# A transformer block with window attention, rebuilt as a pipeline over four groups of 512 tokens, with 64-key score blocks of head pairs and softmax sums by a block-diagonal matmul

## The chip, the cores and the metric

The kernel runs on one core of one Trainium2 chip. The metric is device time in microseconds (us), as the median of several runs. The profile is of one execution; its span, from the first to the last instruction, is 1.7 to 2.1 us shorter than the time of the same run, in every run on record that has both. "Clock" is the mean clock that the throttle granted to the TensorE array, 1.00 being full speed. A run's state is called slow when it is over 1.5% above the fastest of its kernel; ratios use the fast runs alone. Experiments with changed kernels were timed beside the kernel before on the same chip, in three batches on three chips.

Engines: PE is TensorE (PEld its weight loads), ACT is ScalarE, DVE is VectorE, POOL is GpSimd, SP issues the DMAs. PSUM is the memory that matmuls write; an eviction copies from it.

## The reference

One block on 2048 tokens of 512 features: adaptive layer norm, causal attention with a window of 256 and 32 heads of 16, output projection and gated residual, a second adaptive norm, then an MLP that mixes along the *token* axis, again with norm, gate and residual. Cut to what matters:

```python
h = layernorm(x) * (1 + ca) + sa                # modulation from silu(c) @ w_mod
q, k, v = split_heads(h @ wqkv)                 # H = 32 heads of 16
scores = where((q_idx >= k_idx) & (q_idx - k_idx < 256), q @ k.T / 4, -1e9)
x = x + ga * (softmax(scores) @ v) @ wo
h = layernorm(layernorm(x) * (1 + cb) + sb)
u = gelu(einsum('sd,sf->df', h, w1) + b1)       # S = 2048 tokens -> F = 1792
x = x + gb * (u @ w2 + b2).T                    # F -> S
```

## The kernel before

Three stages follow each other. (1) Norm, transposes, value projection and the first query/key projection of all 2048 tokens. (2) Attention, in 8 passes (4 groups of 128 features, even and odd heads) over 16 key blocks of 128; the other 12 projections run in its background. (3) Output projection, norms and MLP, whose two products of 224 matmuls each are called B1 and B2 below. The core of stage 2 (cuts marked):

```python
pending_proj = [(4 * i, g8, tg) for i, (g8, tg) in enumerate(...)]   # 12 projections, one every 4 steps
...
for hs in range(8):                        # 8 passes: (g8, even or odd heads)
    for kb in range(NT):                   # 16 key blocks of 128
        et = epool.tile([P, 4, 3, P], DT.bfloat16, name="et")
        for a in range(2):                 # 4 heads x 3 query blocks: 2 exps of 128 x 768
            nc.scalar.activation(out=et[:, 2*a:2*a+2, 0:nr, :],
                in_=cur[a][:, :, 0:nr*P]..., func=ACT.Exp, scale=SCORE_SCALE)
        cur = emit_scores(ps_s, Ksel, QT[g8], kb + 1, ...)
        while pending_proj and pending_proj[0][0] <= att_step: ...   # 8 matmuls of 512 columns
        att_step += 1
        nc.vector.tensor_tensor(out=et[:, :, 0:3:2, :], ...)         # mask the two edge blocks
        for j in range(4):                 # values, 16 columns of ones beside them: the sums come free
            for kk in kks:
                nc.tensor.matmul(po[32*j:32*j+32, qi, :], lhsT=vaug_lhsT(kk, head), rhs=ering[kk]...)
        if qi == 3: ...                    # VectorE: cast, transpose, reciprocal, multiply, transpose
```

Each 128x768 exp has 3 query blocks of 128, of which the window needs 256 + 128/2 on average; the rest is masked to zero afterwards.

The softmax here doesn't subtract the row's maximum and nothing guards it: scores larger than these inputs give would overflow.

## Time and profile before

| | before |
|---|---|
| time, median of 3 runs before the prediction (4 with the next) | 408.64 us (411.1) |
| span of the profile | 404.0 us |
| stage 1, up to the first exp | 46.8 us |
| stage 2, up to the last value matmul | 222.8 us |
| stage 3 | 134.4 us |

The first view is the page of the kernel before: busy time of each engine, then the granted clock in tenths of full speed in 40 slices of 10.1 us, then three of the costliest groups (line, engine, operation, output and inputs, count | busy us, mean ns of one | idle before it and what ended most of that).

```profile
PE 350.6 (87%) x3713; PEld 168.9 (42%) x3713; DVE 279.5 (69%) x656; ACT 267.8 (66%) x426; POOL 8.7 (2%) x24
...
PEclk9999999699999655555555555569999999999997
...
L317 ACT ACTIVATE et<-pss 128x768 bf16<-128x768 f32 (+2 forms) x256 | 179.5, 779 | 30.4 <-PE psb L347 27.9
L329 DVE TENSOR_TENSOR et<-et,mask_661 128x1024 bf16<-128x1024 bf16 x112 | 75.3, 678 | 25.5 <-ACT et L317 25.0
L347 PE MATMUL psb<-et,VaugT 128*32 128x128 bf16 x1440 | 78.4, 276 | 1.8 <-DVE et L329 0.7
```

The exps are 256 instructions and 179.5 us of ScalarE. Of the 30.4 us that ScalarE sat idle just before an exp, 27.9 were ended by L347, the value matmul that stands ahead of the next scores in PE's queue. PE's own "busy" is no measure of its load, since matmuls overlap (those of 512 columns last 0.38 us in the records and start 0.216 us apart).

The second view cuts the kernel before into its three stages: from : to, length, busy us and instruction count of each engine, then clock, DMA share and GB/s.

```profile
0.00:46.80 46.80, 33.43 (x214) 17.08 (x215) 33.65 (x98) 25.41 (x48) 8.69 (x24) 1.00 0.53 158
46.80:269.60 222.80, 200.21 (x2980) 100.58 (x2978) 161.04 (x307) 185.11 (x270) 0.00 (x0) 0.68 0.01 2
269.60:404.00 134.40, 116.94 (x526) 51.24 (x521) 84.82 (x252) 57.24 (x109) 0.00 (x0) 0.97 0.33 126
```

Attention has ScalarE at 83% (185.11 of 222.80 us) and a mean clock of 0.68. The third view counts only the exps (L317) in stretches of attention of the kernel before.

```profile
46.00:100.00 54.00, 42.02 (x59) 0.94 0.01 2
100.00:145.00 45.00, 36.98 (x55) 0.87 0.01 2
145.00:200.00 55.00, 45.69 (x65) 0.50 0.01 2
200.00:260.00 60.00, 50.42 (x72) 0.50 0.01 2
```

Until about 135 us, projections of full array size fill PE's background and the clock is near 1. When they have run out, it is 0.50 to the end of attention. The exps are about as dense in both halves (0.82 of the time at 100 to 145 us, 0.84 at 200 to 260), from which I concluded, before the prediction, that the clock does not matter here.

### The profile page before, as it was taken

To read this page: it belongs to the slowest core of one execution; us is meant where nothing else is said; L and a number is where in the kernel's file an instruction comes from. 1 tells how busy PE (TensorE), PEld (TensorE's weight loads), DVE (VectorE), ACT (ScalarE), POOL (GpSimd) and SP (SyncE) were. 2 spreads that over 40 slices of the span, in tenths; PEclk is the share of its full clock that TensorE was granted. 3 is DMA by queue.
4 is the path that set the end of the run, shared out by engine and by line. 5 is a ranking of instruction groups with operands and counts; after the bars stand their busy time and mean duration, and the time that the engine had idled before them with its cause. 6 is when DMAs were issued, how large, how long until landed. Compare 5 with 4: busy or idle time off the path is not lost.

```text
span 404.0 us, 8898 instructions
## 1 busy us (share of the span) xinstructions
PE 350.6 (87%) x3713; PEld 168.9 (42%) x3713; DVE 279.5 (69%) x656; ACT 267.8 (66%) x426; POOL 8.7 (2%) x24
## 2 busy tenths in 40 slices
PE   0898997999998898988889988998996799899993
PEld 0543443444444444544444444533342344344441
DVE  6795676688978587757687666679996597522344
ACT  3486588788988888978788878859997554300000
POOL 8000000000000000000000000000000000000000
PEclk9999999699999655555555555569999999999997
DMA  7970000000000000000000000007900592001111
GB/s 221 357 152 0 2 2 2 2 2 2 2 2 2 3 2 2 2 2 2 2 2 2 2 2 2 2 2 287 408 34 0 205 412 112 0 6 48 53 54 53
DMA packets 17169, 24.70 MB, mean 61 GB/s; under 512 B 5096, under 2 KB 12776, under 8 KB 17128
## 3 DMA queue, kind: packets, MB, share of 16 engines
q1 hardware_dynamic: 17128, 24.13, 17.0%
q8 instruction: 29, 0.48, 0.5%
q14 instruction: 12, 0.10, 0.1%
HBM read 22.03 MB, written 2.10 MB: 60 GB/s over the span
## 4 chain that ended last, share of the span: by engine, by line
PE 55%; DVE 21%; ACT 18%; issue 5%; DMA 1%; SPq 0%; ACTq 0%; DVEq 0%
PE pss L289 13%; PE psb L347 13%; ACT et L317 12%; PE py L519 12%; PE pu L499 7%; PE psb L161 3%; DVE ln_stats L455 2%; PE psb L168 2%; DVE ln_stats L436 2%; PE psb L221 2%; DVE et L329 2%; ACT h1T L211 2%; DVE ln_stats L192 1%; PE psb L429 1%; ACT gelu_a L405 1%
## 5 line engine op out<-in xcount | busy, mean ns | idle before, releaser
L317 ACT ACTIVATE et<-pss 128x768 bf16<-128x768 f32 (+2 forms) x256 | 179.5, 779 | 30.4 <-PE psb L347 27.9
L329 DVE TENSOR_TENSOR et<-et,mask_661 128x1024 bf16<-128x1024 bf16 x112 | 75.3, 678 | 25.5 <-ACT et L317 25.0
L347 PE MATMUL psb<-et,VaugT 128*32 128x128 bf16 x1440 | 78.4, 276 | 1.8 <-DVE et L329 0.7
L347 PEld LDWEIGHTS <-VaugT 128*32 128x32 bf16 x1440 | 37.6, 110 | 40.4 <-issue 34.4
L519 PEld LDWEIGHTS <-w2r 128*128 128x128 bf16 x224 | 21.9, 98 | 28.0 <-issue 1.8
L161 PE MATMUL psb<-h1T,wqkv 128*128 128x512 bf16 x64 | 21.5, 398 | 1.2 <-DVE t_1654 L357 0.4
L168 PE MATMUL psb<-h1T,wqkv 128*128 128x512 bf16 x64 | 18.4, 384 | 1.9 <-DVE t_1101 L357 0.4
L499 PEld LDWEIGHTS <-w1r 128*128 128x128 bf16 x128 | 12.5, 98 | 16.6 <-issue 1.2
L221 PE MATMUL psb<-wqkv,h1T 128*128 128x512 bf16 x64 | 17.6, 401 | 1.9 <-ACT QT_196 L165 0.8
L289 PE MATMUL pss<-QT_198,KoT_206 32*128 32x128 bf16 x180 | 16.0, 297 | 3.1 <-ACT et L317 2.9
L289 PE MATMUL pss<-QT_199,KeT_203 32*128 32x128 bf16 x180 | 16.0, 296 | 2.7 <-ACT et L317 2.7
L289 PE MATMUL pss<-QT_198,KeT_202 32*128 32x128 bf16 x180 | 16.0, 296 | 2.7 <-ACT et L317 2.7
L289 PE MATMUL pss<-QT_199,KoT_207 32*128 32x128 bf16 x180 | 16.3, 297 | 2.4 <-ACT et L317 2.2
L289 PE MATMUL pss<-QT_197,KoT_205 32*128 32x128 bf16 x180 | 15.3, 286 | 3.2 <-ACT et L317 3.0
L398 PEld LDWEIGHTS <-w1r 128*128 128x128 bf16 x96 | 9.7, 101 | 19.7 <-issue 10.8
L417 ACT ACTIVATE gelu_sg<-gelu_inner 128x512 bf16<-128x512 bf16 x14 | 8.8, 630 | 11.9 <-DVE gelu_inner L413 11.9
L409 DVE SCALAR_TENSOR_TENSOR gelu_sq<-gelu_a 128x512 bf16<-128x512 bf16 x14 | 9.6, 687 | 7.3 <-ACT gelu_a L405 7.1
L289 PE MATMUL pss<-QT_196,KeT_200 32*128 32x128 bf16 x180 | 11.4, 220 | 3.2 <-ACT et L317 2.4
L289 PE MATMUL pss<-QT_196,KoT_204 32*128 32x128 bf16 x180 | 11.9, 228 | 0.4 <-ACT et L317 0.4
L289 PEld LDWEIGHTS <-KoT_207 32*128 32x128 bf16 x180 | 7.6, 115 | 10.6 <-issue 10.3
L289 PE MATMUL pss<-QT_197,KeT_201 32*128 32x128 bf16 x180 | 11.3, 217 | 0.5 <-ACT et L317 0.2
L289 PEld LDWEIGHTS <-KoT_206 32*128 32x128 bf16 x180 | 7.5, 115 | 9.9 <-issue 9.7
(523 smaller groups left out, 570.0 us busy)
## 6 DMA issues: line engine op xcount, KB each, us to landing
w1r<-in_B_w_dram SPq DMA_DIRECT2D x16, 448.0 KB, 9.0
w2r<-in_B_w_dram SPq DMA_DIRECT2D x14, 512.0 KB, 9.5
wmod<-in_w_mod_dram SPq DMA_DIRECT2D x6, 512.0 KB, 6.1
out_dram<-otile SPq DMA_DIRECT2D x16, 128.0 KB, 1.7
wqkv<-in_A_wqkv_dram SPq DMA_DIRECT2D x4, 384.0 KB, 6.2
wod<-in_A_wo_dram SPq DMA_DIRECT2D x4, 128.0 KB, 3.4
x_64<-in_A_x_dram SPq DMA_DIRECT2D x1, 128.0 KB, 2.1
x_65<-in_A_x_dram SPq DMA_DIRECT2D x1, 128.0 KB, 2.2
```

The source lines that it names most:

```text
L161: nc.tensor.matmul(pq[:], lhsT=wqkv[:, dc, g8 * P : (g8 + 1) * P], rhs=h1T[:, dc, tok], start=(dc == 0), stop=(dc == ND - 1),)
L168: nc.tensor.matmul(pk[:], lhsT=wqkv[:, dc, D + g8 * P : D + (g8 + 1) * P], rhs=h1T[:, dc, tok], start=(dc == 0), stop=(dc == ND - 1),)
L221: nc.tensor.matmul(pv[:], lhsT=h1T[:, dc, tb * P : (tb + 1) * P], rhs=wqkv[:, dc, 2 * D : 3 * D], start=(dc == 0), stop=(dc == ND - 1),)
L289: nc.tensor.matmul(pss[:, jj, r * P : (r + 1) * P], lhsT=Ksel[rows, kb * P : (kb + 1) * P], rhs=qt[rows, qb * P : (qb + 1) * P], start=Tru ...
L317: nc.scalar.activation(out=et[:, 2 * a : 2 * a + 2, 0:nr, :], in_=cur[a][:, :, 0 : nr * P].rearrange("p h (r q) -> p h r q", q=P), func=AC ...
L329: nc.vector.tensor_tensor(out=et[:, :, 0:3:2, :], in0=et[:, :, 0:3:2, :], in1=mask01[:].unsqueeze(1).to_broadcast([P, 4, 2, P]), op=ALU.mult,)
L347: nc.tensor.matmul(po[32 * j : 32 * j + 32, qi, :], lhsT=vaug_lhsT(kk, head), rhs=ering[kk][:, j, r, :], start=(idx == 0), stop=(idx == le ...
L398: nc.tensor.matmul(pu[:, i, :], lhsT=w1r[:, sc, fc * P : (fc + 1) * P], rhs=hb[sc][:], start=(sc == 0), stop=(sc == NT - 1),)
L409: nc.vector.scalar_tensor_tensor(out=sq[:], in0=a[:], scalar=GELU_C0, in1=a[:], op0=ALU.mult, op1=ALU.mult,)
L417: nc.scalar.activation(out=sg[:], in_=inner[:], func=ACT.Sigmoid, scale=GELU_C1)
L499: nc.tensor.matmul(pu[:, i, :], lhsT=w1r[:, sc, fc * P : (fc + 1) * P], rhs=hb[sc][:], start=(sc == 0), stop=(sc == NT - 1),)
L519: nc.tensor.matmul(py[:, tl, :], lhsT=w2r[:, fc, tb * P : (tb + 1) * P], rhs=guT[fc][:], start=(fc == 0), stop=(fc == NF - 1),)
```

## The change

Its intent: do not wait for all projections before attention; give ScalarE fewer and larger exps; let PE make the softmax sums in the layout in which they are needed, so that VectorE need not transpose; do the norms of finished tokens while attention still runs.

- **Groups.** Four groups of 512 tokens. Group G's attention runs while group G+1's projections and group G-1's output projection and norms are issued between its steps.
- **Scores.** A block is 64 keys of an even head on partitions 0 to 63 and of the odd head of the pair on 64 to 127. One row-tiled matmul (on 32 of the array's 128 rows; the value and sum matmuls are column-tiled, on 32 of its columns) makes scores for both heads, up to 320 queries wide. Blocks are packed into chunks of 512 columns: 76 steps of 2 exps of 128x1024 (128x768 in four of them).
- **Sums.** A second matmul with a block-diagonal matrix of ones (scaled by 2^-32) puts each head's sum on the partitions of its values; ScalarE inverts it as exp(-ln z); one VectorE multiply finishes.
- **Engines.** Norm application, value evictions and residuals move to VectorE; the masked key copies to GpSimd; GELU becomes one activation; 1/sqrt becomes exp(-0.5 ln), so attention needs a single activation table.

The diff, cut to its core:

```diff
-            for j in range(4): ... 12 score matmuls of 128 columns, 2 exps of 128x768
+CHUNKS = [[(-2, 0, 3, 0), (-4, 0, 1, 192), (-1, 0, 4, 256)], ...]   # (key block, query, width, column)
+    def emit_exp_mask(tiles, ch, masks):
+        for a in range(2):
+            nc.scalar.activation(out=et[:, 2*a:2*a+2, lo:D], in_=tiles[a][:, :, lo:D],
+                                 func=ACT.Exp, scale=SCORE_SCALE)
...
+            for dst, isv in ((u.x, True), (u.y, False)):
+                for j in range(4):
+                    nc.tensor.matmul(dst[32*j:32*j+32, KB*qs:KB*(qs+nq)],
+                        lhsT=VT[r][:, kbi, 4*u.g8+j, :] if isv else ones_bd[:],
+                        rhs=et[:, j, col:col+KB*nq], ...)
...
-                    nc.vector.tensor_copy(out=t1[:], ...)      # cast, transpose, reciprocal,
-                    nc.vector.transpose(out=t2[:], in_=t1[:])  # multiply, transpose
+        nc.scalar.activation(out=lz[:], in_=u.y[:], func=ACT.Ln)
+        nc.scalar.activation(out=lz[:], in_=lz[:], func=ACT.Exp, scale=-1.0)
+        nc.vector.tensor_tensor(out=OT[u.G % 2][u.g8][:], in0=u.x[:], in1=lz[:], op=ALU.mult)
...
+            post = post_work(u.G - 1) if u.G > 0 else mod_jobs + [early, wod_scale]
+            proj = proj_work(u.G + 1) if u.G + 1 < NG else []
...
-        ... six-step GELU with Sigmoid
+        nc.scalar.activation(out=g[:], in_=pu[:], func=ACT.Gelu_apprx_tanh, bias=b1FM[:, fc:fc+1], scale=1.0)
```

## The prediction

> **What bounds the kernel now.** The slices and the stretch table show three stages: layer norm and projections of all tokens until 47 us, attention until 269 us (first exp to last value matmul), then output projection, norms and MLP until 404 us. In attention ScalarE limits: exps take 179.5 us (256, mean 779 ns) and its busy share is 83 to 90%; the rest is handshakes with PE (groups view: 27.9 us of idle before exps is put down to L347, the value matmul). From 135 us the granted clock is 0.50, once the interleaved projections have run out. After 270 us the chain of waits runs through norm statistics on VectorE; PE is dense only from 330 us (352 matmuls of 512 columns, 0.216 us start to start: 76 us).
>
> **What the change does, costed from the trace.**
>
> 1. Exp columns: 184,320 now; after, 76 steps of 2 x 1024 (less in four), about 154,000. Back-to-back exps take 0.545 us (512) and 0.757 us (768), so 1024 is estimated at 0.97 us: 147 us in place of 179.5.
> 2. Added on ScalarE: Ln and Exp per unit to invert the sums, 16 x 2 x 0.6 = 19 us. With query evictions (12 x 0.6) and the norms' Ln/Exp (5 us) about 180 us in attention. Value evictions, output copies and norm applications leave ScalarE.
> 3. VectorE loses transposes, casts, reciprocals and merges (75 us) and masks less (57 for 82 us), but gains h1T, value evictions, residual adds: 150 to 170 us inside attention, close to ScalarE. GpSimd takes the masked key copies; the Trainium skill (SBUF — State Buffer, "Who interferes with whom") says GpSimd and some VectorE modes exclude each other. In this trace one 128x512 tensor-scalar took 2.50 us beside GpSimd memsets, its neighbours 0.40. I allow 10 us.
> 4. PE: the sums become a second matmul, 24 for 12 output matmuls a step. Warm about 1.9 us a step with drains and background work, below ScalarE's 2.35. Projections run through groups 0 to 2, so the clock should stay near 1.0 until the last group.
> 5. Start: only group 0 is projected first: first exp near 30 us, not 47.
> 6. Tail: norms of groups 0 to 2 move into attention. After it stay 448 MLP matmuls x 0.216 = 97 us, output projection 3, handover and last output 7, visible weight loading 2.
> 7. Table loads (1.28 us) shrink to two or three: Ln and Exp share a set (ScalarE: Activation LUTs, "Table sets"). GELU is one 0.68 us activation, off the path.
>
> **Sum.** 30 + 180/0.86 = 209 + 109 = 348 us of span; timed runs are 4.6 us above the span now, so 352.
>
> I predict 351 us, 80% range 325 to 382; faster by over 2% 0.93, within 2% 0.03, slower 0.04.
>
> **What would show it.** First exp near 30 us; about 150 exps, mean 0.97 us, 147 us; ScalarE 80 to 90% busy from 30 to 240 us; clock 1.0 there except at the end; PE over 95% busy for the last 100 us.
>
> **What would make it wrong.** In-order ScalarE stalls: the Ln of the sums waits for the last value matmul, the query copy for its projection, the norm's Ln for four statistics (4 x 0.8 us); exposed each time, 40 to 70 us come on top. Score tiles in PSUM fall from three to two. VectorE could become the limit if value evictions or GpSimd collisions cost more. A cold clock throughout attention would make PE the limit (3.3 us a step, total near 400). Packing better than 86% gives 330.

## The result and the profile after

| | before | after |
|---|---|---|
| time, median of 4 runs | 411.1 us | 325.63 us (324.87 to 326.79) |
| span | 404.0 | 323.2 |
| up to the first exp | 46.8 | 24.05 |
| attention | 222.8 | 188.3 |
| after attention | 134.4 | 110.8 |

The ratio of after to before is 0.7987, with a 95% interval of 0.7938 to 0.8036. Here and below a ratio is the mean time of one kernel's fast runs over that of the other's in the same rounds, so it is not quite the ratio of the medians quoted. Two of the four runs of the kernel before (413.56 and 419.05 us) were slow and are left out: 407.8 us before, 325.7 after.

The page of the kernel after, the same lines. L404 is now the exp, L411 and L416 are the masks, L435 the value (pox) and sum (poy) matmuls.

```profile
PE 274.4 (85%) x3277; PEld 133.9 (41%) x3313; DVE 209.4 (65%) x487; ACT 182.3 (56%) x241; POOL 39.2 (12%) x57
...
PEclk9999999999998999979999997679999999999998
...
L404 ACT ACTIVATE et<-pss 128x1024 bf16<-128x1024 f32 (+1 forms) x152 | 147.0, 1024 | 21.6 <-PE pss L390 20.8
L435 PE MATMUL poy<-et,ones_bd 128*32 128x128 bf16 (+4 forms) x768 | 43.1, 263 | 0.2
L411 DVE TENSOR_TENSOR et<-et,maskt 128x256 bf16<-128x256 bf16 (+2 forms) x104 | 33.4, 344 | 12.1 <-ACT et L404 11.8
...
L416 DVE TENSOR_TENSOR et<-et,maskt 128x512 bf16<-128x512 bf16 x48 | 20.5, 427 | 13.5 <-ACT et L404 12.7
```

The exps take 147.0 us, as forecast, and the clock stays near 1 except for two dips of 3.4 us (at 102 and 139 us) and near the end of attention. The masks cost 53.9 us (33.4 + 20.5) in place of 82. The three stages of the kernel after:

```profile
0.00:24.05 24.05, 9.63 (x110) 6.34 (x111) 19.00 (x37) 2.69 (x5) 15.51 (x27) 1.00 0.90 254
24.05:212.37 188.32, 163.97 (x2718) 82.83 (x2744) 146.50 (x366) 167.27 (x216) 23.71 (x31) 0.95 0.08 28
212.37:323.20 110.83, 100.81 (x449) 44.70 (x458) 43.93 (x86) 12.37 (x21) 0.00 (x0) 0.97 0.31 119
```

ScalarE is busy for 167.27 of 188.32 us of attention, 89%, and the mean clock there is 0.95. So the 80.8 us of span come in three parts: 22.8 at the start, 34.5 in attention, 23.6 after it. The exps by stretch, as shown above for the kernel before:

```profile
34.00:60.00 26.00, 19.83 (x23) 1.00 0.40 143
60.00:90.00 30.00, 24.46 (x26) 1.00 0.01 3
...
120.00:150.00 30.00, 24.39 (x26) 0.94 0.01 2
...
180.00:212.40 32.40, 27.81 (x29) 0.84 0.01 2
```

I had feared that ScalarE would stand still at each norm statistic in its queue. The waits of ScalarE in the kernel after between 60 and 180 us (who waited <- for whom: us in total, times, longest) say that it does not:

```profile
ACT et L404 <- PE pss L390: 9.6, 12, 1.5
ACT rs L240 <- DVE mv L238: 0.6, 1, 0.6
```

Only 0.6 us went to the statistics; the idle time is waiting for scores, that is for PE. Over the whole of attention the sums' Ln waited 1.1 us for value matmuls, and the query copies 2.6 us for their projections.

### The profile page after: what moved, and what is told of

Its sections match the earlier page's. It is cut to its first block, busy times and chain, and to the rows that moved or that the text cites. A ratio compares the mean times of both kernels' runs of the same rounds, so it can differ in the third digit from the quotient of the medians.

```text
span 323.2 us, 7621 instructions
## 1 busy us (share of the span) xinstructions
PE 274.4 (85%) x3277; PEld 133.9 (41%) x3313; DVE 209.4 (65%) x487; ACT 182.3 (56%) x241; POOL 39.2 (12%) x57
## 4 chain that ended last, share of the span: by engine, by line
PE 43%; DVE 24%; ACT 23%; issue 6%; DMA 2%; SPq 0%
ACT et L404 17%; PE py L578 15%; PE pu L570 8%; PE pss L390 5%; DVE st L237 4%; PE pox L435 3%; DVE VT_147 L323 3%; DVE xn L245 3%; PE pu L562 2%; PE pv L313 2%; PE pa L344 2%; ACT lz L446 2%; PE poy L435 2%; ACT lz L447 2%; DMA w1b<-in_B_w_dram 2%
## 5 line engine op out<-in xcount | busy, mean ns | idle before, releaser
L404 ACT ACTIVATE et<-pss 128x1024 bf16<-128x1024 f32 (+1 forms) x152 | 147.0, 1024 | 21.6 <-PE pss L390 20.8
L435 PE MATMUL poy<-et,ones_bd 128*32 128x128 bf16 (+4 forms) x768 | 43.1, 263 | 0.2
L411 DVE TENSOR_TENSOR et<-et,maskt 128x256 bf16<-128x256 bf16 (+2 forms) x104 | 33.4, 344 | 12.1 <-ACT et L404 11.8
L416 DVE TENSOR_TENSOR et<-et,maskt 128x512 bf16<-128x512 bf16 x48 | 20.5, 427 | 13.5 <-ACT et L404 12.7
L435 PE MATMUL pox<-et,VT_147 128*32 128x320 bf16 (+4 forms) x352 | 20.2, 263 | 3.7 <-DVE OT_1_155 L448 1.5
L435 PEld LDWEIGHTS <-ones_bd 128*32 128x32 bf16 x768 | 19.6, 99 | 7.1 <-issue 3.6
L240 ACT ACTIVATE rs<-mv,eps_t 128x4 f32<-128x4 f32 x12 | 3.6, 298 | 20.4 <-DVE mv L238 20.3
L435 PEld LDWEIGHTS <-VT_147 128*32 128x32 bf16 x352 | 9.1, 96 | 13.8 <-issue 12.9
L299 DVE CAST kb<-pk 128x512 bf16<-128x512 f32 x16 | 11.0, 687 | 4.8 <-PE pk L294 4.7
L435 PE MATMUL pox<-et,VT_148 128*32 128x320 bf16 (+4 forms) x208 | 11.0, 261 | 1.1 <-DVE OT_1_151 L448 0.6
L323 DVE CAST VT_147<-pv 64x512 bf16<-64x512 f32 x16 | 11.0, 689 | 0.8 <-PE pv L313 0.5
L435 PE MATMUL pox<-et,VT_149 128*32 128x320 bf16 (+4 forms) x208 | 11.2, 262 | 0.0
L313 PE MATMUL pv<-wqkv,h1T_159 128*64 128x256 bf16 x128 | 10.7, 294 | 0.0
L447 ACT ACTIVATE lz<-lz 128x512 f32<-128x512 f32 x16 | 10.5, 658 | 0.0
```

The lines of the kernel that those rows point to most:

```text
L313: nc.tensor.matmul(pv[KB * par : KB * (par + 1), i, :].rearrange("p (a d) -> p a d", d=DH), lhsT=h1T[r2][:, dc, tok], rhs=wv[:, dc, par, : ...
L323: nc.vector.tensor_copy(out=dst, in_=src)
L404: nc.scalar.activation(out=et[:, 2 * a : 2 * a + 2, lo:D], in_=tiles[a][:, :, lo:D], func=ACT.Exp, scale=SCORE_SCALE,)
L411: nc.vector.tensor_tensor(out=dst, in0=dst, in1=msk.to_broadcast([P, 4, KB * mn]), op=ALU.mult,)
L416: nc.vector.tensor_tensor(out=dst, in0=dst, in1=maskt[:, m0 : m0 + 2, :].unsqueeze(1).to_broadcast([P, 4, 2, KB]), op=ALU.mult,)
L435: nc.tensor.matmul(dst[32 * j : 32 * j + 32, KB * qs : KB * (qs + nq)], lhsT=VT[r][:, kbi, 4 * u.g8 + j, :] if isv else ones_bd[:], rhs=et ...
```

## The experiments

Twelve runs were made, all with correct results; two of them are the kernel after again, as a control. The batch of b_spread, a_proj_early, a_post_late and a_exp_extra had no control on its chip, and only two of its seven runs of the kernel before were fast (405.36 and 411.25). What these kernels lose is therefore given as a range, against the ratios 0.8098 to 0.7987 that the kernel after has elsewhere. "The kernel after" is the base of those whose names begin with a, "the kernel before" of those with b.

### b_spread: the clock, first attempt

```diff
-    pending_proj = [(4 * i, g8, tg) for i, (g8, tg) in enumerate(
+    pending_proj = [(8 * i, g8, tg) for i, (g8, tg) in enumerate(
```

> The kernel before, with its twelve background projections issued every 8 attention steps in place of every 4, so that the full-array matmuls (and with them the full clock) last until about step 96 of 128, not 48. Theory A (ScalarE's exp columns limit attention in both kernels, the clock hardly matters): the exps took 0.84 of the time at clock 1.0 (100 to 130 us) and 0.83 at clock 0.5 (145 to 260 us), so the time stays within 2% (400 to 415 us), though the granted clock in attention rises from 0.68 to over 0.85. Rival B (the fall of the clock to 0.5 cost the kernel before much of what the change gained): with the clock kept up, at least 12 us less (below 396 us).

Measured: 436.63 us (434.06 to 437.07), ratio 1.0681 (1.0531 to 1.0831). Both theories missed: it got slower. The page's clock line of b_spread, and then the exps by stretch, show why:

```profile
PEclk9999955555555555555555555556999899999998
```

```profile
46.00:100.00 54.00, 38.26 (x54) 0.57 0.01 2
100.00:145.00 45.00, 31.06 (x47) 0.50 0.01 2
145.00:200.00 55.00, 37.29 (x53) 0.50 0.01 1
200.00:260.00 60.00, 45.39 (x65) 0.50 0.01 2
```

The projections, spread thinner, no longer held the clock: it fell to 0.50 at about 55 us, not 135, and stayed there, so 53 exps ran between 145 and 200 us where the kernel before ran 65 at that same clock. At half clock *with* projections to do, PE is the limit: between 145 and 260 us ScalarE waited 17.7 us before an exp or a query copy in the kernel before, 17.4 of them for the value matmul L347, and 28.4 us here, 22.2 of them for L347. The arithmetic was unchanged; 4 steps of spacing made the difference. That the exps had been equally dense in both halves of the kernel before looks like a coincidence of two loads: projections at full clock, none at half clock.

### b_warm: the clock, second attempt

```diff
+                if att_step >= 48 and att_step % 4 == 0:
+                    pd = ps_big.tile([P, 4 * P], DT.float32, name="psb")
+                    for rep in range(8):
+                        nc.tensor.matmul(pd[:], lhsT=wqkv[:, rep % ND, 0:P], rhs=h1T[:, rep % ND, 0:4*P],
+                                         start=(rep == 0), stop=(rep == 7))
                 att_step += 1
```

> The kernel before, with eight full-array 512-column matmuls of no use every fourth step from step 48 on, in place of the projections that have run out: the granted clock should stay at 1.0 through attention, at the price of 20 x 8 x 0.216 = 35 us of PE. If the half clock cost the second half of attention nothing (ScalarE's exps were as dense at 0.5, 36 per 30 us, as at 1.0 beside projections, 37 per 30 us): within 2% of the kernel before. If the half clock alone held the second half back: faster by 2% or more in spite of the useless work. If PE was full there: slower by 3% or more.

Measured: ratio 0.9735 (0.9666 to 0.9804). Its fast runs took 394.8 and 395.1 us at a mean clock of 0.98, where the fast runs of the kernel before took 404.4 to 408.2 at 0.80 to 0.81. Useless matmuls made the kernel 2.65% faster: the half clock did hold back the second half. The gain rests on two runs: two of the four were slow (407.2 and 414.0 at clock 0.93 and 0.91) and left out; the profile is of one of those, in which the clock dropped for a while earlier on (0.50 from 61 to 82 and from 130 to 160 us). Its exps by stretch still show the late part, where the clock was 1:

```profile
145.00:200.00 55.00, 43.20 (x64) 0.86 0.01 2
200.00:260.00 60.00, 53.33 (x79) 1.00 0.01 2
```

From 200 to 260 us 79 exps ran, where the kernel before had 72 at clock 0.50.

### a_proj_early: projections ahead of attention again

```diff
-    QT = [[... for g in range(ND)] for r in range(2)]
+    QT = [[... for g in range(ND)] for r in range(3)]
     for w in pw[1:]:
         w()
+    for G in (1, 2):
+        for w in proj_work(G):
+            w()
-            proj = proj_work(u.G + 1) if u.G + 1 < NG else []
+            proj = proj_work(3) if u.G == 2 else []
```

> The kernel after, with the projections of groups 0, 1 and 2 all before attention (group 3's stays in group 2). Theory A: the first dense exps start about 25 us later, and the attention of groups 0 and 1, freed of that work, is 4 to 8 us shorter: total +17 to +23 us (343 to 349). Rival B (clock): without full-array matmuls in groups 0 and 1 the granted clock falls to 0.5 there, and attention gets longer in place of shorter: total more than +28 us.

Measured: 353.6 us (352.72 to 354.88), ratio 0.8663 (0.8547 to 0.8778); that is 7.0 to 8.5% or 23 to 28 us more than the kernel after, at the border of the two theories. The clock did fall in the four stretches of 20 us from 80 to 160 us (a_proj_early; its clock is the third number from the right), where the kernel after has 0.91 to 1.00:

```profile
80.00:100.00 20.00, 18.09 (x268) 8.04 (x269) 8.75 (x24) 18.45 (x23) 0.00 (x0) 0.75 0.50 184
100.00:120.00 20.00, 18.32 (x270) 8.01 (x267) 12.81 (x36) 17.46 (x23) 0.00 (x0) 0.74 0.01 2
120.00:140.00 20.00, 19.22 (x264) 7.73 (x262) 11.33 (x35) 17.88 (x23) 0.00 (x0) 0.60 0.01 2
140.00:160.00 20.00, 19.84 (x242) 8.25 (x241) 12.48 (x32) 16.53 (x20) 0.00 (x0) 0.63 0.01 2
```

How the loss divides can be read from the starts of the same exps in both traces. The first exp is no later (23.1 us), but the 20th starts at 76.4 us in place of 52.2: 24 us are lost by the later start. From there to the 134th exp (214.8 us, 189.9 in the kernel after) both need the same time, 138.4 and 137.7 us. So the later start is nearly all of the loss, as reckoned; what was missed is that attention, freed of the projections of groups 1 and 2, got no faster. That the lower clock ate what their absence saved is likely, but not separated.

### a_post_late: output projection and norms behind attention again

```diff
-            post = post_work(u.G - 1) if u.G > 0 else mod_jobs + [early, wod_scale]
+            post = [] if u.G > 0 else mod_jobs + [early, wod_scale]
-    for w in post_work(NG - 1):
-        w()
+    for G in range(NG):
+        for w in post_work(G):
+            w()
```

(and four output buffers in place of two.)

> The kernel after, with the output projection and norms of groups 0 to 2 taken out of attention and done after it, together with group 3's. Theory A: inside attention this work was hidden behind ScalarE; after it, it costs about 16 us of VectorE per group (as group 3's does, 214 to 230 us), of which B1 hides a part. Tail +25 to +35 us, attention -3 to -8 us, total +20 to +30 (345 to 356 us). Rival: in attention this work cost about as much as it takes, through ScalarE waits for norm statistics; then the total stays within 5 us of 325.6.

Measured: 339.63 us (338.69 to 340.87), ratio 0.832 (0.8207 to 0.8433); that is 2.7 to 4.2% or 9 to 14 us more than the kernel after. Neither number was right. The stages of a_post_late (its last value matmul is at 200 us):

```profile
24.00:201.00 177.00, 159.18 (x2725) 80.94 (x2723) 121.89 (x287) 165.35 (x206) 23.01 (x31) 1.00 0.09 30
201.00:337.00 136.00, 109.99 (x482) 47.75 (x479) 71.60 (x165) 14.44 (x31) 0.00 (x0) 0.94 0.25 97
```

The edit did less than it was meant to: 30 of the 64 matmuls of the output projection (from 160 us on), and the first statistics, were moved by the compiler into the last group of attention. The part after attention grew by about 25 us, as expected; but attention lost 12 us, more than expected. With that work moved, ScalarE is 93% busy over attention, and 97 to 100% between 60 and 180 us (19.4 to 20.0 of each 20 us), at clock 1.00. So the background norms are not free: in the kernel after they take some 12 us of attention to save about 25 later. Part of the 12 us may be the clock: the kernel after has the two dips to half clock, with 2.7 us of ScalarE's idle time inside them, and a_post_late has none before 204 us.

### a_exp_extra: more ScalarE work, which went elsewhere

```diff
+        nc.scalar.activation(out=xout[:], in_=xin[:], func=ACT.Exp, scale=1.0)   # constant 128x256 input
         for col, stride, m0, mn in masks:
```

> The kernel after, with one more exp of 128x256 on constant data in each of the 76 steps, its result never read: about 0.35 us each, 27 us of ScalarE in all. Theory A (ScalarE limits attention): +20 to +28 us (346 to 354). Rival C (PE with its mode changes limits as much as ScalarE): most of it is hidden, +12 us or less.

Measured: 332.94 us (329.81 to 336.38, the last a slow run, which is also the one profiled), ratio 0.8129 (0.7953 to 0.8304), 0.4 to 1.8% or 1 to 6 us more. That looks like the rival's answer, but the experiment did not do what it was meant to. The extra exps depended on nothing, and the order of the queues is decided at compile time: 41 of the 76 were put before 24 us, where ScalarE is idle, and none after 76 us. It says nothing about the limit of attention.

### a_control, a_exp_tied and a_sum_twice: is ScalarE the limit?

a_control is the kernel after. a_exp_tied gives the extra exp an input that exists only in its step:

```diff
+        nc.scalar.activation(out=xout[:], in_=tiles[1][:, 1, D - 256 : D], func=ACT.Exp, scale=SCORE_SCALE)
         for col, stride, m0, mn in masks:
```

a_sum_twice issues each sum matmul twice with halved weights:

```diff
-    nc.gpsimd.memset(ones_bd[0:KB, 0:DH], ZSCALE)                        # and the other block
+    nc.gpsimd.memset(ones_bd[0:KB, 0:DH], ZSCALE / 2)
-            for dst, isv in ((u.x, True), (u.y, False)):
+            for di, (dst, isv) in enumerate(((u.x, True), (u.y, False), (u.y, False))):
-                        start=u.first, stop=stop, ...
+                        start=u.first and di < 2, stop=stop and di != 1, ...
```

> The kernel after, unchanged, beside the other three on the same chip: 325 us within 2, ratio to the kernel before 0.79 to 0.81.

> The extra exp of 128x256 again, but now reading the second score tile of its step, so that it cannot be issued early into ScalarE's idle start as the 76 of the first attempt were. About 0.33 us each, 25 us of ScalarE inside attention, which the kernel after spends 91% busy. Theory A (ScalarE limits attention): +18 to +28 us over the control. Rival C (PE limits as much): +12 us or less.

> The kernel after, with every block-diagonal sum matmul issued twice and its weights halved (same result): 768 more column-tiled matmuls, at full clock about 16 us of PE. Theory A: PE has slack at full clock, +5 us or less over the control, exp share unchanged. Rival C (PE limits as much): +12 to +18 us.

| | time, us | ratio to before | over the control |
|---|---|---|---|
| a_control | 328.44 (327.41 to 329.81) | 0.8098 (0.8049 to 0.8147) | |
| a_exp_tied | 339.16 (337.39 to 339.7) | 0.8346 (0.8291 to 0.8401) | +10.7 |
| a_sum_twice | 337.13 (336.3 to 337.81) | 0.831 (0.827 to 0.835) | +8.7 |

The extra exps, now all in place, and the doubled sums: first the line of the extra exp and the page's engine line of a_exp_tied, then the engine line of the control.

```profile
L408 ACT ACTIVATE xout<-pss x76: 373/420/632, 25.4 to 224.8; 128x256 bf16<-128x256 f32 x76
```

```profile
PE 285.3 (84%) x3276; PEld 137.1 (41%) x3313; DVE 211.2 (62%) x487; ACT 202.6 (60%) x317; POOL 38.7 (11%) x57
```

```profile
PE 276.1 (85%) x3277; PEld 134.4 (41%) x3313; DVE 209.7 (64%) x487; ACT 182.7 (56%) x241; POOL 39.3 (12%) x57
```

The control missed its own forecast of 325 us within 2. ScalarE got 19.9 us more to do (202.6 - 182.7), and the time rose by 10.7 us, 54% of it. Some 16 us more on PE (an estimate: 76 chunks of 512 columns at 0.216 us) cost 8.7 us. By the expectations the first falls on rival C's side (12 us or less) and the second between the two; with "ScalarE alone is the limit", the first would have cost nearly 20 us and the second nearly nothing. In the profiled executions attention itself grew by 12.7 and 11.8 us, 64% and 72% of the added work. The clock blurs the first a little: near the end of attention it was half for 31 us in a_exp_tied and for 17 us in the control; but up to the 114th exp, before that, a_exp_tied had already lost 7.3 us. Attention after the change is limited by both engines in turn. The stretches of 60 us of the control and the two others show how the extra work is taken up; the first fence is a_control, then a_exp_tied, then a_sum_twice.

```profile
60.00:120.00 60.00, 52.49 (x891) 26.52 (x892) 45.88 (x112) 54.02 (x70) 11.12 (x14) 0.97 0.01 2
120.00:180.00 60.00, 52.24 (x900) 26.82 (x909) 45.24 (x114) 54.55 (x70) 6.44 (x8) 0.97 0.01 2
```

```profile
60.00:120.00 60.00, 52.34 (x841) 25.74 (x841) 45.31 (x110) 57.34 (x90) 9.46 (x12) 0.97 0.01 2
120.00:180.00 60.00, 52.32 (x848) 26.02 (x853) 42.33 (x103) 56.31 (x88) 7.49 (x10) 0.94 0.01 2
```

```profile
60.00:120.00 60.00, 51.11 (x1028) 27.52 (x1036) 44.47 (x108) 50.50 (x65) 7.97 (x10) 0.94 0.01 2
120.00:180.00 60.00, 50.72 (x1074) 27.86 (x1083) 41.05 (x102) 49.15 (x63) 8.68 (x12) 0.94 0.01 2
```

With more exps ScalarE fills its gaps, from 90 to 95% of the 120 us. With more sums ScalarE waits longer for scores, and its share falls to 83%.

### a_gelu_old, a_memset_late, a_both and a_control2: start and tail

a_control2 is the kernel after again. a_gelu_old puts the old GELU (Identity, two VectorE steps, Sigmoid, two VectorE multiplies per chunk) back in place of the one activation. a_memset_late and a_both:

```diff
-    for r in range(3):
-        nc.gpsimd.memset(VT[r][:], 0.0)
+    nc.gpsimd.memset(VT[0][:], 0.0)
     pw = proj_work(0)
 ...
     emit_masks()
+    for r in (1, 2):
+        nc.gpsimd.memset(VT[r][:], 0.0)
```

```diff
 # a_both has, besides, the work pool outside the memory that attention gives back to w1 and w2
-    work = att.enter_context(tc.tile_pool(name="work", bufs=3))
+    work = ctx.enter_context(tc.tile_pool(name="work", bufs=3))     # ahead of att
```

> The kernel after, unchanged, beside the other three on the same chip: 324 to 329 us.

> The kernel after with the old six-step GELU (two ScalarE passes, four on VectorE) in place of the one GELU activation. If GELU is off the path, as predicted: 0 to 3 us more than the control, the little that there is at the handover from B1 to B2, where the last chunk's chain is about 3.1 us and not 1.1. If it was part of the gain: 8 us or more.

> The kernel after, with the memsets of the second and third value buffer (3.5 us each on GpSimd) moved behind the masks. In the trace after, one 128x512 tensor-scalar on VectorE took 3.77 us while such a memset ran, its neighbours 0.40, and the modulation, transposes and first projection waited in line behind it. If that wait is on the path: 2.5 to 4 us less than the control, first exp near 21 us. Rival: the start is bound by the landing of the weights or by PE, and nothing is gained (within 1 us).

> The late memsets, and the work pool kept out of the memory that w1's second half takes, so that its load need not wait for the last norm of group 3 (230.5 us) but only for the last reads of the attention buffers (near 219). B1 takes 50.1 us where its 224 matmuls need 48.4, so this part can give 1.7 us at most: 3 to 6 us below the control in all.

| | time, us (6 runs) | ratio to before |
|---|---|---|
| a_control2 | 327.85 (324.58 to 329.46) | 0.8011 (0.7957 to 0.8066) |
| a_gelu_old | 327.4 (326.72 to 330.77) | 0.8039 (0.799 to 0.8089) |
| a_memset_late | 329.2 (327.22 to 329.62) | 0.8057 (0.8013 to 0.81) |
| a_both | 325.4 (323.75 to 326.8) | 0.7973 (0.7929 to 0.8018) |

**GELU** is off the path: no difference clear of the noise, although VectorE has 20 us more to do between 222 and 275 us (35.3 for 15.2). The change of GELU brought no gain that these runs can show.

**The memsets.** The expected wait was there and was removed, and nothing was gained. VectorE's time order at the start, first in the kernel after, then in a_memset_late (start, duration, engine, line, operation, and in brackets the idle time before it and what ended it):

```profile
8.45 3.77 DVE L245 TENSOR_SCALAR xn<-x_65,mv,rs 128x512 bf16<-128x512 bf16 x1 [0.60 <-ACT rs L241]
12.15 0.47 DVE L245 TENSOR_SCALAR xn<-x_66,mv,rs 128x512 bf16<-128x512 bf16 x1
...
13.44 0.14 DVE L178 COPY sT<-st_ps 128x4 bf16<-128x4 bf16 x1
```

```profile
8.45 1.53 DVE L245 TENSOR_SCALAR xn<-x,mv,rs 128x512 bf16<-128x512 bf16 x4 [0.60 <-ACT rs L241]
...
10.16 0.14 DVE L178 COPY sT<-st_ps 128x4 bf16<-128x4 bf16 x1
...
14.28 0.69 DVE L237 BATCH_NORM_STATS2 st<-x 128x6 f32<-128x512 bf16 x1 [2.66 <-DMA x<-in_A_x_dram]
14.89 0.53 DVE L274 TENSOR_SCALAR h1T<-pt,modFM 128x512 bf16<-128x512 bf16 x1
```

One normalization of 128x512 took 3.77 us beside a GpSimd memset; with the memset moved, four took 1.53 us together and the modulation came 3.3 us earlier. But next in VectorE's queue stood the statistics of a tile of group 1 (L237), 2.66 us early for its DMA, and only behind it the evictions of group 0 (L274). The first exp came at 24.5 us, not earlier. The wait was turned into another one.

**Both.** With the pool kept apart, the load of w1's second half was issued at 221.6 us, in the control at 232.5, and PE ran its last 448 matmuls without a stall: from the first start to the last, B1 took 48.1 us (222.6 to 270.7), 50.6 in the control (221.6 to 272.2). The median is 2.4 us below the control's, less than the 3 to 6 expected, and the intervals of the ratios overlap: no difference is shown. Its ratio is the lowest, but not clearly better than that of the kernel after.

## Why the prediction was right

The time, 325.63 us, lies in the range of 325 to 382, but only 0.6 us above its lower end; the forecast of 351 was 25 us too high. That it fell inside is luck. The direction, the exps and the tail were right; the start and two terms of the attention sum were mis-sized, all three the same way, and one claim about the limit was only half right.

| term of the sum | predicted | measured |
|---|---|---|
| first exp | 30 us | 24.05 |
| ScalarE work in attention | 180 | 167.3 |
| packing | 0.86 | 0.888 (167.3 / 188.3) |
| attention | 209 | 188.3 |
| after attention | 109 | 110.8 |
| timed run over span | 4.6 | 2.4 (1.7 in the same run) |

The 4.6 compared the median of several runs with the span of one execution, which by the 1.7 was a faster one.

1. **Exp columns: right.** 152 exps and 147.0 us, against "147 us in place of 179.5".
2. **"Added on ScalarE ... about 180 us in attention": mis-sized by 13 us, which is 15 of the 21 us in attention (12.7 / 0.86).** I added up durations. Those were right: Ln 0.613 and Exp 0.658 (16 each), 15 query copies of 0.61, 9 pairs for the norms of about 0.5 together make 33.9 us (of which the last Exp, 0.66, falls behind the stage). But successive activations overlap: two exps in a row take about 1.94 us where one takes 1.02. With exps on either side each small activation costs less than its duration, and 20.3 us (167.3 - 147.0) is what they add. The Trainium skill says so (ScalarE: Activation LUTs, "What ACT_TABLE_LOAD costs": "Back-to-back ACTIVATEs overlap by ≈ 93 ns"), and this trace agrees: 2 x 1.02 - 1.94 = 0.10 us. At the borders of the small activations of the stage the overlaps in the records add up to 12.5 us (101 borders, 0.12 us each), which is what was missing. I had used start-to-start times for the exps and durations for the rest.
3. **Packing: 6 of the 21 us.** In-order waits, which I feared at 40 to 70 us, stayed away: 0.6 us for norm statistics between 60 and 180 us, and in all of attention 1.1 us for the sums' Ln and 2.6 us for query copies.
4. **"PE ... below ScalarE's 2.35", that is, ScalarE limits: half right.** Extra ScalarE work costs 54% of itself, extra PE work about as much of itself. The margin forecast between the two was not there: by the records PE is busy for 164.0 us of attention, 2.16 us a step and not 1.9, ScalarE for 167.3, 2.20 and not 2.35. Without the background norms ScalarE is 97 to 100% busy (a_post_late); with them the two take turns.
5. **Clock: right that it would stay up; its worth was missed.** The prediction gives the clock no share of the gain, and the reading behind that (equal exp density at both clocks) was mistaken. Holding the clock up by useless work brings the kernel before from about 406 to 395 us (b_warm); thinning its projections costs 28 us (b_spread).
6. **Start: 6 us better than reckoned,** since the first scores need only the first query and key projection and are issued ahead of the others; the first steps then run with gaps (4 exps in the first 10 us).
7. **Tail: right,** 110.8 for 109, with PE 93% busy over the last 100 us (93.6 of 100.2) and not over 95%.
8. **Tables and GELU: right.** The loads fell from five to two, each 1.283 us in both traces. That Ln and Exp share a table set, as the Trainium skill says (ScalarE: Activation LUTs, "Table sets"), agrees with the trace after: no load stands between its Ln and Exp activations. GELU is off the path (a_gelu_old).

Where the 81 us come from: 23 at the start and 24 in the tail through the pipeline, which a_proj_early (24 us lost at the start) and a_post_late (25 us lost after attention) bear out; for the 35 in attention the experiments point to two causes. Taking the exps back would cost about 0.54 x 32.5 = 17 us, an estimate from a_exp_tied's rate (21 us by the 64% of the profiled executions); the clock was worth about 11 us in the kernel before (b_warm, which pays for its useless matmuls besides). Neither was undone in the kernel after, and the two need not add up. What remains is not separated: the transposes taken off VectorE, larger instructions with fewer handshakes, or the interplay of the two causes.

## What to carry to other kernels

Where the full-array matmuls stand can move the clock, and with it the time: with the same arithmetic the kernel before got 7% slower when they were spread, and it got 2.7% faster by useless ones. What density holds the clock was not found here, so look at the granted clock of each stage before you move any. When you cost an engine's queue, add start-to-start times, not durations. And an experiment that adds work must tie it to the place where it is meant to hurt, or a compile-time scheduler will hide it in the first idle gap.

## What the Trainium skill lacked or had wrong

- TensorE: Matmul & The Clock Gate ("What's actually happening" and "HAM oscillation") ties the half clock to an idle PE and gaps of over about 3.4 us; a section after these adds frequent short idle times, with a clock that oscillates. Here the half clock holds without a break for 230 us in b_spread (0.50 from 60 to 290 us) while PE is busy for 92% of the time (211 of 230 us in the records, whose matmul ends are modelled). In these traces row- and column-tiled matmuls alone kept the full clock for 16 us (86 to 102 us in the kernel after, then a dip) and in no run for more than 19 us, and in the kernel before it was 0.50 as long as they were alone (145 to 260 us). What density of full-array matmuls holds it was not found: 58 in 54.6 us went with 1.00 in the kernel before (79 to 134 us) and 98 in 246 us with 0.50 in b_spread, but 12 in 20.5 us with 1.00 in a_proj_early (155 to 175 us) and 23 in 30.7 us with 0.50 in b_warm (130 to 160 us). The two levels that the page gives, half and full, are the ones that the stretches show (0.50 and 1.00).
- TensorEngine Tiling (Array Packing) ("Key Properties") says that a change of tiling mode drains the array, without a cost. In the kernel after the weight loads of the scores were idle for 39.6 us in 134 instances before they could go, under "issue" (0.15 to 0.90 us each, median 0.26), 92 of them behind a weight load of another shape; that the drain is the cause is an inference, and as weight loads overlap matmuls, not all of it is lost time.
- SBUF — State Buffer ("Who interferes with whom") is borne out: 3.77 us for 0.40 beside a 3.52 us memset, and 0.4 again with the memset moved. What it does not say is that removing such a block may gain nothing, as a_memset_late shows.
- No page says that compilation may move added instructions far ahead of their place in the text: 41 of 76 extra exps ran before 24 us.
